# The branch ahead of a fused attention and expert kernel moved behind it, and the work planned anew

## The chip, the cores and the metric

The kernel runs on one core of one Trainium2 chip. The metric is the device time of one execution in microseconds; three timed executions of the kernel before gave a median of 732.55 us (731.89 to 733.72). Besides these there is one profiled execution, from which every number about single instructions comes.

## What is computed

The reference is an attention with a sliding window and a few global keys, followed by a gated product of two projections and an output projection:

```python
# q, k, v: (4, 8, 768, 64); n_global = 8, n_local = 96
scores = scale * np.matmul(q, k.transpose(0, 1, 3, 2))
is_global = pos[None, :] < int(n_global)
is_local = (rel >= 0) & (rel < int(n_local))      # rel = row - column
keep = is_global | is_local
dist = np.where(is_global & ~is_local, float(n_local), np.abs(rel))
scores = np.where(keep, scores - slopes * dist, -1e9)
a = softmax(scores)                               # with 1e-9 added to the sum
x = (a @ v) as 3072 rows of 512
out = ((x @ w_a) * (x @ w_b)) @ w_out             # d_ff = 1536
```

The two counts, n_global and n_local, are inputs of the program (64-bit integers in HBM), and so are the weights, which arrive as 64-bit floats and are turned into a high and a low float part on the chip. A program must therefore be right for other counts as well. The kernel has a fast path, which covers n_global up to 8 and n_local from 1 to 97, and a general path for everything else. The inputs of all runs here are covered by the fast path.

## The kernel before, in words

**The start.** `build` (L1401) loads the counts into a tile `nv` on SP's queue, and the first tile of packed queries and keys, `raw0`, in four pieces on the queues of SP and ScalarE (`build_first`, L1387). GpSimd writes positions, VectorE makes them into distances (`build_positions`, L1349). `load_flag` (L1341) has each of the five engines read the four 32-bit words of the counts from HBM into registers. `build_counts` (L1328) turns the 64-bit counts into floats on VectorE with four small operations (L1334 to L1337), and `build_masks` (L1374, six VectorE operations, L1379 to L1384) makes the two masked distance tiles `rel` and `col` with them. Then comes `tc.If(fast > 0)` (L1419): every engine works out the condition in its own registers and branches; the fast path is the first arm, the general path the `Else` arm (L1422).

**The fast path.** Its work is cut into eight units. Unit 0 holds the first block of 128 query rows of each of the four batches, the others two or three blocks each. For each unit there is an attention part, and then the projections (`moe`, L1000) in 12 steps, one for each 128 of d_ff. While unit u goes through its projections, the attention of unit u + 1 is done beside it. Unit 0's attention (`first`, L853) has nothing to hide beside. It goes through four pairs of heads in the order of `FIRST` = (1, 0, 2, 3); for each pair two `quad`s (L802), each of which has score matmuls on PE (L821), the subtraction of the scaled distances with a row minimum on VectorE (L659), the exponential on ScalarE (L676), a normalization (L708 or L710), a transposition on PE (L735), a copy out of PSUM, and the product with V (L787). Each head other than head 2 needs its own multiple of the two distance tiles; these are made by `scale_dists` (L635, one narrow and one wide operation for each head, L641), on VectorE or GpSimd. The weights of each of the 12 steps come as two loads on SP's queue (L473) and are converted by ScalarE and VectorE (`load_w`, L455), 768 columns at a time; the projections of unit 0 can't go on without them.

**What sets the order.** Every piece of work is an `Op` with a due time and a cost for each engine that can do it. `Schedule.order` (L266) plays the program through with these costs, gives each operation an engine where there is a choice, and writes down one order; the instructions are then emitted in exactly that order (`run`, L1121). The due times are first shifted at random by the numbers in `MOVES` (L79), each of which stands for one set of shifts, for operations of about the first two units. In the plan all engines are free at time 0.

**The first loads.** `fetch_first` (L541) gives the four raw tiles and the four V tiles of unit 0 due times ahead of everything else, each V tile next to its raw tile; they lie in memory that later holds the weights of the last steps (`w8` to `w11`). The weight tiles are in one pool (L407), and its memory starts where temporary tiles of the mask operations had been.

**The end.** The last unit's results are copied out of PSUM and stored by SP, and a last half by ScalarE's queue (L1113). Then each engine leaves the arm of the branch, past the general path, and all meet in a closing barrier (recorded at L1402).

Of the kernel before, what the change touches and what calls it, by code (L numbers as in the profile page):

```python
# [47 lines left out]

HOMES = "kk sm raw hh v wm hl xh xl o qh pf ql t"
PAD = 40  # L50
# [28 lines left out]
MOVES = (1010, 1025, 1037, 1048, 1089, 1106, 1156, 1251, 1276, 1371, 1475, 1603, 1662, 1754, 1881, 11792, 12402, 7, 26, 46, 60, 85, 142, 169, 213, 252, 392, 531, 549, 595, 835, 995, 2161, 2240, 11001)  # L79
TRACE = False  # L80
LAGS = {"pe": 200.0, "act": 270.0, "dve": 230.0, "pool": 290.0, "dma": 2300.0}
BIG = float(2**38)
# [143 lines left out]
class Schedule:  # L226
# [39 lines left out]
    def order(self, ops, dues):  # L266
# [5 lines left out]
        free = {e: 0.0 for e in self.SYNC}  # L272
# [36 lines left out]
        for op in ops:  # L309
            if not op.before:  # L310
                arrive(op)
        while len(out) < len(ops):
# [48 lines left out]
            elif kind == 1:  # L361
                arrive(op)
            else:
# [26 lines left out]
class Fast:  # L390
# [28 lines left out]
    def sbuf(self, shape, dtype, tag, name, bufs=1):  # L419
        return self.plan.buf(self.sp[tag], shape, dtype, tag, name, bufs=bufs)  # L420

# [33 lines left out]
    def load_w(self, f, due):  # L455
# [3 lines left out]
        for g in range(2):  # L459
            raw = self.plan.buf(self.wp, [P, 2 * WN], I32, f"w{f}_{g}", f"wr{f}_{g}")  # L460
            w = self.plan.buf(self.wp, [P, 2 * WN], F32R, f"w{f}_{g}", f"wt{f}_{g}")
# [79 lines left out]
    def fetch_first(self, c, due):  # L541

        pl = PLANS[0]
        v = self.plan.buf(self.wp, [P, 2 * WN], F32, f"w{NF - 1 - c}_1", f"v0_{c}")
        nv = 2 * pl.nv * D
        if c != FIRST[0]:
            raw = self.plan.buf(self.wp, [P, 2 * WN], F32, f"w{NF - 1 - c}_0", f"raw0_{c}")
# [87 lines left out]
    def scale_dists(self, h, due, wide):  # L635
        rel, col = self.dists
        b, n = self.negs[h // 4], (h % 4) * 3 * P
        for src, at, w, when in ((col, 2 * P, P, due), (rel, 0, 2 * P, wide)):
            self.plan.op(
                when,  # L640
                lambda e, src=src, at=at, w=w: self.engine(e).tensor_scalar_mul(  # L641
                    b[:, n + at : n + at + w], src[:, :w], 2.0 ** (2 - h)
# [5 lines left out]
                pool=pool(w) * 0.5,  # L648
            )
# [471 lines left out]
    def run(self):  # L1121
# [23 lines left out]
        with self.tc.manual_schedule():  # L1145
            for op in order:
# [181 lines left out]
def build_counts(nc, pool, nv):  # L1328

    words = nv.bitcast(I32).rearrange("p (n two) -> p n two", two=2)  # L1330
    low, high = words[:, :, 0], words[:, :, 1]
    nf = pool.tile([P, 2], F32, name="nf")
    t = pool.tile([P, 2], F32, name="nt")
    nc.vector.tensor_scalar(t, low, 0.0, None, op0=ALU.is_lt)  # L1334
    nc.vector.tensor_copy(nf, low)
    nc.vector.tensor_tensor(t, t, high, op=ALU.add)
    nc.vector.scalar_tensor_tensor(nf, t, float(2**32), nf, op0=ALU.mult, op1=ALU.add)  # L1337
# [3 lines left out]
def load_flag(nc, ns):  # L1341

    _, words = nc.values_load_multi_w_load_instructions(ns.bitcast(I32)[0:1, 0:4])
    g, g_high, l, l_high = words
    small = ((g >> 4) | g_high | (l >> 7) | l_high) == 0
    return small & (g <= G) & (l >= 1) & (l <= LW + 1)
# [54 lines left out]
def build(nc, a, out):  # L1401
    with tile.TileContext(nc) as tc, ExitStack() as ctx:  # L1402
        cp = ctx.enter_context(tc.tile_pool(name="c", bufs=1))
        with tc.manual_schedule(), tc.tile_pool(name="tmp", bufs=1) as tp:
# [3 lines left out]
            spare = cp.tile([P, PAD], F32, name="spare")  # L1408
            nc.gpsimd.memset(spare, 0.0)
            nc.scalar.activation(spare, spare, AF.Exp)  # L1410
# [8 lines left out]
        with tc.If(fast > 0) as branch:  # L1419
            with inner:  # L1420
                main.run()
# [75 lines left out]
```

## Time and profile before

| | |
|---|---|
| median of three runs | 732.55 us |
| the profiled execution's own time | 731.68 us |
| its span, first to last instruction | 729.8 us |
| mean granted clock of TensorE | 0.999 |
| busy: PE, VectorE, ScalarE, GpSimd | 708.6, 483.1, 353.1, 5.9 us |

In the rows of the profile PE is TensorE's matmuls, PEld its weight loads, DVE VectorE, ACT ScalarE, POOL GpSimd and SP SyncE. A q behind an engine's name (ACTq, SPq) means its sequencer, which issues DMAs, reads registers and branches; such records are not counted as busy. A row such as `8.38 0.40 ACT L676 ...` gives a start and a length in us, the engine and the line; what stands in brackets is how long the engine sat idle before it, and what ended that. A busy PE is not necessarily at its peak, since its matmuls overlap in their records.

### The profile page before, as it was taken

Reading aid. Unit: us, or ns where it says so; the run is one execution under the profiler, and the core shown is the slowest. Engines: PE = TensorE matmul, PEld = TensorE weight load, DVE = VectorE, ACT = ScalarE, POOL = GpSimd, SP = SyncE. Lnnn points to the kernel's source line nnn. Section 1 sums busy time; section 2 is a strip of 40 time slices with the busy share of each in tenths; the row PEclk is TensorE's granted clock in tenths of the full one; section 3 lists DMA queues with packets and bytes.
Section 4 is the critical chain, followed back from the end, with each engine's and each line's share of the span. In section 5 each row is a group of like instructions: output and inputs, shape, how many; then the busy total and the mean of one; then the engine's idle time right before and its main releaser. Section 6 shows DMA issues by size and latency. Waiting matters only on the chain.

```text
span 729.8 us, 12598 instructions
## 1 busy us (share of the span) xinstructions
PE 708.6 (97%) x4356; PEld 639.2 (88%) x4356; DVE 483.1 (66%) x1560; ACT 353.1 (48%) x907; POOL 5.9 (1%) x16
## 2 busy tenths in 40 slices
PE   5899999999999999999999999999999999999996
PEld 4577777899899999999899999998999999999996
DVE  6999999779975873587726967278662896321111
ACT  5999776364553552555426544263443554221111
POOL 3000000000000000000000000000000000000000
PEclk9999999999999999999999999999999999999999
DMA  7899100134543343134331343224432243110001
GB/s 269 316 380 364 41 17 28 42 101 127 170 137 81 90 129 108 64 89 125 89 104 65 106 129 108 65 85 106 135 101 86 65 128 88 45 44 1 1 1 48
DMA packets 38552, 78.06 MB, mean 107 GB/s; under 512 B 8528, under 2 KB 21072, under 8 KB 38480
## 3 DMA queue, kind: packets, MB, share of 16 engines
q1 hardware_dynamic: 28960, 67.33, 28.8%
q10 hardware_dynamic: 9520, 9.84, 5.3%
q8 instruction: 36, 0.59, 0.3%
q14 instruction: 36, 0.29, 0.1%
HBM read 51.97 MB, written 6.29 MB: 80 GB/s over the span
## 4 chain that ended last, share of the span: by engine, by line
PE 84%; DVE 5%; ACT 3%; DMA 3%; ACTq 2%; issue 1%; SPq 1%; DVEq 0%; POOL 0%; POOLq 0%
PE p L1042 49%; PE acc L1060 24%; PE pa L787 5%; PE ps L953 4%; DMA pf<-wm 3%; ACTq L766 2%; DVE t L659 1%; ACT t L676 1%; DVE wm L752 1%; ACT wr L516 1%; PE pt L735 1%; PE ps L821 1%; SPq L766 1%; DVE kk L447 1%; PE acc_2b L1060 1%
## 5 line engine op out<-in xcount | busy, mean ns | idle before, releaser
L1042 PE MATMUL p<-xh,wt 128*128 128x384 f32 (+2 forms) x1488 | 419.5, 337 | 1.4 <-ACT raw L437 0.9
L1042 PEld LDWEIGHTS p<-xh,wt 128*128 128x128 f32 x1488 | 271.0, 188 | 15.2 <-ACT raw L437 1.9
L1042 PE MATMUL p<-xl,wt 128*128 128x384 f32 (+2 forms) x816 | 269.7, 340 | 0.7 <-ACT xl L437 0.5
L1060 PE MATMUL acc<-wt,hh 128*128 128x512 f32 (+1 forms) x576 | 203.4, 390 | 0.0
L1042 PEld LDWEIGHTS p<-xl,wt 128*128 128x128 f32 x816 | 153.4, 188 | 10.8 <-ACT xl L437 0.8
L1060 PEld LDWEIGHTS acc<-wt,hh 128*128 128x128 f32 x576 | 108.3, 188 | 20.0 <-issue 1.6
L1081 DVE TENSOR_TENSOR raw<-p,raw 128x384 f32<-128x384 f32 (+2 forms) x96 | 52.9, 551 | 90.5 <-PE p L1042 89.7
L676 ACT ACTIVATE t<-t,sm 128x232 f32<-128x232 f32 (+1 forms) x120 | 55.3, 464 | 116.7 <-DMA pf<-wm 71.3
L1060 PE MATMUL acc<-wt,hl 128*128 128x512 f32 (+1 forms) x288 | 111.7, 388 | 0.0
L437 ACT COPY raw<-p 128x384 f32<-128x384 f32 (+2 forms) x71 | 34.4, 485 | 122.3 <-PE p L1042 116.2
L447 DVE TENSOR_TENSOR hl<-raw,hh 128x384 fp32r<-128x384 f32 (+2 forms) x96 | 52.8, 550 | 11.1 <-ACT hh L437 10.4
L1060 PEld LDWEIGHTS acc<-wt,hl 128*128 128x128 f32 x288 | 54.2, 188 | 6.6
L659 DVE CUSTOM_DVE_ANT_0 t<-ps,rel 128x232 f32<-128x232 f32 x74 | 28.8, 389 | 39.2 <-PE ps L953 38.4
L447 DVE TENSOR_TENSOR kk<-raw,kk 64x348 fp32r<-64x348 f32 x96 | 49.6, 516 | 3.6 <-ACT kk L437 0.5
L437 ACT CAST hh<-raw 128x384 fp32r<-128x384 f32 (+2 forms) x72 | 37.3, 519 | 19.8 <-DVE raw L1081 19.6
L787 PE MATMUL pa<-pf,v 128*64 128x128 f32 x640 | 41.5, 278 | 1.7 <-ACT pf L437 1.4
L787 PEld LDWEIGHTS pa<-pf,v 128*64 128x64 f32 x640 | 35.9, 138 | 7.2 <-issue 3.5
L953 PE MATMUL ps<-kk,qh 128*128 128x232 f32 x144 | 39.8, 277 | 1.5 <-DVE sm L659 1.5
L708 ACT ACTIVATE wm<-wm,sm 128x232 f32<-128x232 f32 x58 | 27.9, 487 | 24.6 <-DVE sm L698 23.9
L953 PE MATMUL ps<-kk,ql 128*128 128x232 f32 x144 | 39.5, 274 | 0.0
L676 ACT ACTIVATE wm<-wm,sm 128x232 f32<-128x232 f32 x72 | 34.7, 483 | 5.7 <-DVE sm L659 5.1
L708 ACT ACTIVATE t<-t,sm 128x232 f32<-128x232 f32 (+1 forms) x76 | 34.6, 477 | 5.1 <-DVE sm L698 4.0
(84 smaller groups left out, 687.4 us busy)
## 6 DMA issues: line engine op xcount, KB each, us to landing
wr<-wts SPq DMA_DIRECT2D x24, 768.0 KB, 10.9
raw<-qkv SPq DMA_DIRECT2D x48, 366.0 KB, 3.0
v<-qkv SPq DMA_DIRECT2D x24, 384.0 KB, 3.2
pf<-wm ACTq DMA_DIRECT2D x192, 48.0 KB, 2.0
pf<-wm SPq DMA_DIRECT2D x192, 48.0 KB, 1.9
out<-o SPq DMA_DIRECT2D x23, 256.0 KB, 2.0
v<-qkv SPq DMA_DIRECT2D x8, 256.0 KB, 3.9
raw<-qkv SPq DMA_DIRECT2D x3, 512.0 KB, 8.0
```

What stands on the lines that cost most here:

```text
L437: self.nc.scalar.copy(out(), src())
L447: lambda e: self.engine(e).tensor_sub(out(), a(), b()),
L516: lambda e, low=low: nc.scalar.activation(low(), low().bitcast(U32), AF.Copy, scale=2.0**-29),
L659: lambda e, j=j, o=o, w=w, neg=neg, at=at: nc.vector.tensor_tensor_reduce(t[:, o : o + w], ps[:, o : o + w], neg[:, at : at + w], -scale, ...
L676: lambda e, j=j, o=o, w=w: nc.scalar.activation(t[:, o : o + w], t[:, o : o + w], AF.Exp, bias=sm[:, j : j + 1], scale=-1.0, accum_out=sm[ ...
L708: nc.scalar.mul(t[:, o : o + w], t[:, o : o + w], r)
L766: lambda e, out=out, src=src: self.queue(e).dma_start(out(), src()),
L787: nc.tensor.matmul(pa[D * s : D * s + D, i * P : i * P + P], v[:, v0 : v0 + D], probs[s, i][1](c), start=c == 0, stop=c == len(slots) - 1,)
L953: nc.tensor.matmul(ps[:, :w], q[:, i * P : i * P + P], kk[:, k0 : k0 + w], start=m == 0, stop=m == 1,)
L1042: nc.tensor.matmul(p[:, :T], wt(), b[:, b0 : b0 + T], start=c == 0 and n == 0, stop=c == NCC - 1 and n == 2,)
L1060: nc.tensor.matmul(acc[:, :n], hs[:, i * P : i * P + P], wt(), start=f == 0 and k == 0, stop=f == NF - 1 and k == 2,)
L1081: lambda e, asb=asb, pb=pb: nc.vector.tensor_mul(asb[:, :T], pb[:, :T], asb[:, :T]),
```

## The change

The test moves from ahead of the fast path to behind it, and a few things that hang on that are changed with it:

- `load_flag` and the branch at the start are gone. The fast path is emitted without a condition.
- The masks take only the lower words of the counts, by one cast (`build_low`); the high words no longer enter the masks.
- When 95% of the plan's operations have been emitted, `late()` puts in seven small VectorE operations which make the full counts and one flag in SBUF, and has ScalarE, VectorE, GpSimd and SP read the flag into a register. TensorE reads it behind its last matmul.
- Behind the fast path stands `tc.If(flag == 0)` with the general path in it, told to fall through on the side where the condition is false. For counts that aren't covered the general path writes the output again.
- The plan knows at which times the engines become free (`BEGIN`), ScalarE may do the scaling of the distances, the V tiles' due times lie two loads later, and `MOVES` has 15 other numbers in place of 35. The plan's order is thereby another one throughout.
- Every weight tile has its own pool; the pools are opened with the tiles of step 4 first, and those of steps 0 to 3 last.
- The operand of the first exponential, which only loads its table, is one column of the limits tile and not a tile of 40 columns.

```diff
+BEGIN = {"pe": 4700.0, "act": 5200.0, "dve": 5100.0, "pool": 5200.0, "dma": 2400.0}
...
-        free = {e: 0.0 for e in self.SYNC}
+        free = dict(BEGIN)
...
+        for n, at in enumerate(sorted(BEGIN.values())):
+            heappush(heap, (at, 3, n, None))
...
-        self.wp = ctx.enter_context(tc.tile_pool(name="w", bufs=1))
+        tags = [f"w{(f + 4) % NF}_{g}" for f in range(NF) for g in range(2)]
+        self.wp = {tag: ctx.enter_context(tc.tile_pool(name=tag, bufs=1)) for tag in tags}
...
-            due + 1, lambda e: self.copy_in(v, nv, VOFFS[0][c]), writes=[v], dma=nv * 4 * P / 360.0
+            due + 2 * LOAD + 1,
+            lambda e: self.copy_in(v, nv, VOFFS[0][c]),
...
-                lambda e, src=src, at=at, w=w: self.engine(e).tensor_scalar_mul(
-                    b[:, n + at : n + at + w], src[:, :w], 2.0 ** (2 - h)
+                lambda e, out=out, src=src, by=2.0 ** (2 - h), w=w: (
+                    self.nc.scalar.mul(out(), src[:, :w], by)
+                    if e == "act"
+                    else self.engine(e).tensor_scalar_mul(out(), src[:, :w], by)
                 ),
...
+                act=act(w),
...
-            for op in order:
+            for n, op in enumerate(order):
+                if n == int(LATE * len(order)):
+                    late()
                 op.emit(op.engine)
...
+def build_low(nc, pool, nv):
+    nf = pool.tile([P, 2], F32, name="low")
+    nc.vector.tensor_copy(nf, halves(nv)[0])
+    return nf
...
+class Covered:
...
+    def early(self):
+        self.counts()
+        v, ok = self.nc.vector, self.ok
+        v.tensor_tensor(ok, self.nf, self.lim, op=ALU.is_le)
+        v.scalar_tensor_tensor(
+            ok[:, 0:1], self.nf[:, 1:2], 1.0, ok[:, 0:1], op0=ALU.is_ge, op1=ALU.mult
+        )
+        v.tensor_mul(self.flag, ok[:, 0:1], ok[:, 1:2])
+        self.handles = self.load([e for e in mybir.ALL_ENGINES if e != mybir.EngineType.PE])
+
+    def value(self):
+        handles = self.handles + self.load([mybir.EngineType.PE])
+        return self.nc.snap(bass.RegisterHandles(handles))
...
-            fast = load_flag(nc, a["ns"])
-            nf = build_counts(nc, cp, nv)
-            build_masks(nc, rel, col, first, t, nf)
-        inner = ctx.enter_context(ExitStack())
-        main = Fast(inner, tc, a["qkv"], a["wts"], out, raw0, (rel, col, ident))
-        with tc.If(fast > 0) as branch:
-            with inner:
-                main.run()
-        with branch.Else():
+            build_masks(nc, rel, col, first, t, build_low(nc, cp, nv))
+        covered = Covered(nc, cp, nv, lim)
+        with ExitStack() as inner:
+            Fast(inner, tc, a["qkv"], a["wts"], out, raw0, (rel, col, ident)).run(covered.early)
+        with tc.If(covered.value() == 0, preferred_fallthrough_block=False):
             with ExitStack() as inner:
-                General(
-                    inner, tc, a["qt"], a["kt"], a["v"], a["wts"], out, (nf, ident)
-                ).run()
+                General(inner, tc, a["qt"], a["kt"], a["v"], a["wts"], out, (covered.nf, ident)).run()
```

More of the change, by code (lines that the diff above doesn't have):

```diff
@@ L49 @@
 HOMES = "kk sm raw hh v wm hl xh xl o qh pf ql t"
-PAD = 40
 START = 52000
@@ L1325, in run, with halves @@
             self.batch(b)
-def build_counts(nc, pool, nv):
+def halves(nv):
     words = nv.bitcast(I32).rearrange("p (n two) -> p n two", two=2)
[L1331 to L1337, printed above, removed]
-    return nf
@@ L1341, in load_flag, with build_limits @@
[L1341 to L1346, printed above, removed]
+    return words[:, :, 0], words[:, :, 1]
+def build_low(nc, pool, nv):
+    nf = pool.tile([P, 2], F32, name="low")
+    nc.vector.tensor_copy(nf, halves(nv)[0])
+    return nf
+def build_limits(nc, pool):
+    lim = pool.tile([P, 2], F32, name="lim")
+    nc.gpsimd.memset(lim[:, 0:1], float(G))
+    nc.gpsimd.memset(lim[:, 1:2], float(LW + 1))
+    return lim
```

43 lines of the change are left out of this document (33 added, 10 removed).

## The prediction

> **What bounds the kernel now.** I read the page's head first, then the busy time by stages, then the first microseconds in order of time, then the tail and the waits of TensorE.
>
> ```profile
> span 729.8 us, 12598 instructions
> ```
> ```profile
> 0.00:5.00 5.00, 0.00 (x0) 0.00 (x0) 1.58 (x9) 1.52 (x2) 1.30 (x10) 1.00 0.49 105
> 5.00:10.00 5.00, 2.90 (x23) 2.65 (x24) 4.08 (x29) 1.62 (x9) 4.17 (x5) 1.00 0.66 228
> 10.00:15.00 5.00, 4.46 (x28) 3.03 (x26) 4.05 (x31) 4.11 (x20) 0.09 (x1) 1.00 1.02 376
> 15.00:41.00 26.00, 21.15 (x146) 13.71 (x146) 25.26 (x100) 26.00 (x80) 0.37 (x1) 1.00 0.85 325
> 41.00:60.00 19.00, 18.78 (x95) 15.02 (x96) 19.00 (x41) 19.00 (x35) 0.00 (x0) 1.00 1.01 407
> 60.00:120.00 60.00, 60.00 (x298) 47.10 (x297) 59.23 (x113) 45.24 (x83) 0.00 (x0) 1.00 0.28 102
> 200.00:690.00 490.00, 488.45 (x3049) 455.80 (x3048) 294.98 (x1004) 207.03 (x559) 0.00 (x0) 1.00 0.31 89
> ```
> In the second fence the columns behind the stretch and its length are the busy times of PE, PEld, DVE, ACT and POOL, then the granted clock, the DMA share and GB/s. From 41 us on PE is the bound: it idles 0.22 us to 60, nothing to 120, and 1.55 us in the 490 behind 200. Before 41 it is not: it is busy 28.51 of 41 us. There VectorE and ScalarE are full from 15 us on (25.26 and 26.00 of 26), with the softmax of the first unit and the first weights' conversion. So what the change can win at the front is what it lets these two engines start earlier; the long middle belongs to PE and its work is untouched. The third place is behind PE's last matmul.
>
> **The front, step by step.**
>
> ```profile
> 0.74 0.39 SPq L1406 DMA_DIRECT2D nv<-ns  x1
> ...
> 1.19 1.20 SPq L1397 DMA_DIRECT2D raw<-qkv  x2
> ...
> 3.79 0.17 DVE L1334 TENSOR_SCALAR nt<-nv 128x2 f32<-128x2 int32 x1 [2.07 <-DMA nv<-ns]
> ...
> 4.19 0.16 DVE L1337 SCALAR_TENSOR_TENSOR nf<-nt,nf 128x2 f32<-128x2 f32 x1
> 4.47 0.34 DVE L1379 TENSOR_SCALAR after<-rel,nf 128x224 f32<-128x224 f32 x1
> ...
> 5.09 2.08 PE L821 MATMUL ps<-raw 64*128 64x128 f32 x16 [5.09 <-DMA raw<-qkv]
> ...
> 5.50 0.35 SPq L562 DMA_DIRECT2D raw<-qkv  x1
> ...
> 6.55 1.77 DVE L641 TENSOR_SCALAR negs<-col 128x128 f32<-128x128 f32 x7 [0.92 <-DVE col L1384]
> ...
> 8.04 0.28 DVE L659 CUSTOM_DVE_ANT_0 t<-ps,col 128x128 f32<-128x128 f32 x1
> ...
> 8.38 0.40 ACT L676 ACTIVATE t<-t,sm 128x128 f32<-128x128 f32 x1 [4.85 <-DVE sm L659]
> ...
> 9.80 0.64 DVE L641 TENSOR_SCALAR negs<-rel 128x256 f32<-128x256 f32 x2
> ```
> ```profile
> L1419 DVEq ALU_OP  x12: 47/53/58, 5.5 to 6.4; - x12
> ...
> L1419 ACTq COMPARE_BRANCH  x2: 45/46/47, 4.8 to 724.4; - x2
> L1419 PEldq COMPARE_BRANCH  x2: 92/1914/3737, 4.9 to 721.2; - x2
> L1419 SPq COMPARE_BRANCH  x2: 43/48/53, 5.1 to 724.5; - x2
> L1419 DVEq COMPARE_BRANCH  x2: 55/56/57, 6.4 to 723.5; - x2
> ```
> The first fence is the timeline (start, duration in us, engine, line; in brackets the idle time before and what ended it), the second the source view of the branch (ns, minimum, median and maximum; then first and last start).
>
> *The branch on VectorE.* It does its twelve register operations and its compare only when its masks are issued, from 5.5 to 6.4 us, and the 0.92 us of idle time at 6.55 is that. All of it goes.
>
> *The counts.* Today the masks wait for three further operations: the cast at the second place, then L1336, then L1337, and L1379 starts 0.28 us behind L1337's start. With the cast alone L1379 starts 0.28 us after the cast. The cast can start where L1334 starts now, 3.79, so L1379 at 4.07 and not 4.47: 0.40 us earlier. The four operations with the high words go to the last unit, below.
>
> So VectorE is free at 6.55 − 0.92 − 0.40 = 5.23 us, 1.32 us earlier. Seven narrow scalings stand before its first L659 today. If they all stay, L659 starts at 8.04 − 1.32 = 6.72. If they don't, the scores are the bound: PE starts at 5.09 for the landing of raw, its 16 records for the two quads last 2.08 us, so the first quad is there at 5.09 + 1.04 = 6.13. The first L659 thus moves by 1.32 to 1.91 us. I take 1.8: ScalarE, which may now do scalings, sits idle until 8.38, and the first two L659 read the unscaled distance, so little need stand ahead.
>
> *The nine scalings on VectorE* (1.77 + 0.64 = 2.41 us) may go to ScalarE. What ScalarE does before its first exponential costs nothing; that is 8.38 − 1.8 = 6.6 less 5.2, so 1.4 us, or four or five of them at the 0.40 of an activation of this size. What is taken from VectorE helps by at most half, since copies and normalizations can then be shared anew between two full engines: 0 to 1.2 us, and I take 0.6 as half the scalings move. If ScalarE does them later than its first exponential, they cost it 0.4 each and the term is nought or below: with seven of them behind it, 2.8 − 1.2 = 1.6 us lost.
>
> *The first loads.*
>
> ```profile
> SPq L562 <- DVE rel L1382: 0.3, 1, 0.3
> ```
> SP has issued raw0 at 1.19 + 1.20 = 2.39 us, then reads the counts and branches, and issues its next load at 5.50, the last 0.3 us of it waiting for a mask operation whose memory the load's tile takes over. The weight pools are now opened with w4 ahead, so that this memory falls to a tile that is loaded later. So the load can come at 2.4, with the V tiles each behind the next raw tile. PE waits for a load once, at the very start; no later idle row of it in these 41 us names one. So 3.1 us earlier loads are worth nothing by themselves; they are what keeps up with softmax work that starts 1.8 us sooner, in a stretch where DMA is at 1.02. PE's own start stays at 5.09: it waits for raw0, whose issue isn't moved.
>
> Front: 1.8 + 0.6 = 2.4 us; bounds 1.3 − 1.6 = −0.3 and 1.9 + 1.2 = 3.1.
>
> **The test at 95%.** Seven VectorE operations on 128x2 (0.16 to 0.17 each by the rows above, 1.2 us), and a register read on four engines that waits for them.
>
> ```profile
> 699.96 0.48 ACT L437 COPY raw<-p 128x384 f32<-128x384 f32 x1 [4.55 <-PE p L1042]
> ...
> 700.55 0.56 DVE L1081 TENSOR_TENSOR raw<-p,raw 128x384 f32<-128x384 f32 x1 [4.56 <-PE p L1042]
> ```
> ```profile
> L1343 SPq TENSOR_LOAD <-ns x1: 503/503/503, 3.7 to 3.7; - x1
> ...
> L1343 PEldq TENSOR_LOAD <-ns x1: 1762/1762/1762, 1.8 to 1.8; - x1
> ```
> Queued behind the waiting read are ScalarE's copy of p, VectorE's product and, on SP, stores. In the last unit's steps both engines idle 4.55 us of each; 1.2 and a read of 0.5 to 1.8 us fit (4.55 − 3.0 = 1.5 left), so 0. Without that cover PE would lose up to 3.0 us once. PE's own read comes behind its last matmul.
>
> **The tail.**
>
> ```profile
> L1402 SPq EVENT_SEMAPHORE  x8: 17/28/28, 728.6 to 729.7; - x8
> ...
> L1402 DVEq DRAIN  x2: 10/34/57, 726.8 to 729.3; - x2
> L1402 ACTq DRAIN  x2: 8/38/67, 728.5 to 729.3; - x2
> ```
> ```profile
> 723.98 0.39 ACTq L1113 DMA_DIRECT2D out<-o  x1
> ```
> ```profile
> L1113 SPq DMA_DIRECT2D out<-o x24: 332/343/502, 152.1 to 724.0; - x24
> ```
> ```profile
> out<-o ACTq DMA_DIRECT2D x1, 128.0 KB, 3.1
> out<-o SPq DMA_DIRECT2D x1, 128.0 KB, 3.4
> ```
> The path ends with the last stores: 723.98 + 3.1 = 727.1, and on SP 724.0 + 3.4 = 727.4. But the engines leave the fast arm by jumping over the general path, and then nothing is recorded for a while: VectorE from its compare at 723.5 to 726.8, ScalarE from 724.4 to 728.5, SP from 724.5 to 728.6, and PE's jump itself is a record of 3.74 us. VectorE has no store to wait for, and its gap is 3.3 us, so this is the jump and not the landing. SP and ScalarE are done with it 1.2 us behind the landing, and the closing barrier then takes 729.8 − 728.6 = 1.2. With the general path behind and the covered side falling through, the barrier can begin at 727.4: 1.2 us gained; 0 if a jump remains. I take 1.2, because all four gaps have one size, whether a store stands before them or not.
>
> [...]
>
> **Sum.** 2.4 + 0 + 1.2 = 3.6 us. The profiled execution took 731.68 us (its span 729.8, and 1.9 around it), so 728.1; the median of the runs is 732.55, 0.87 above it, so 728.95, say 729.0.
>
> **The rivals.**
>
> *A. The exit still jumps.* Then ScalarE and SP fetch after their last store as today, and only the front is left: 732.55 − 2.4 = 730.2. For it: the general path has to lie somewhere. Against: the test names the side that falls through. If a wait for the stores also came ahead of such a jump, the end would be 727.4 + 4.1 + 1.2 = 732.7 of span, 2.9 later, and front and tail nearly cancel at 733.0. Together 0.14. [...]
>
> *B. The front is not won.* PE becomes the bound at 41 us only because two engines are full till then, and VectorE stays full to 120. If scalings on ScalarE land among its exponentials (2.8 us, above), only the tail is left: 732.55 − 1.2 = 731.4. For it: ScalarE is the fuller one from 15 to 41. Against: the new start times let it do them before 6.6 us. 0.13.
>
> *C. Slower: the order written anew makes PE wait in the middle.* Other start times and other shifts of due times give another order over the first two units' 24 steps.
>
> ```profile
> 41.22 0.50 PE L1042 MATMUL p<-xh,wt 128*128 128x512 f32 x1 [0.65 <-ACT raw L437]
> ```
> ```profile
> PE ps L953 <- DVE sm L659: 1.5, 3, 0.7
> PE p L1042 <- ACT raw L437: 0.3, 1, 0.3
> PE p L1042 <- DVE raw L439: 0.2, 1, 0.2
> ```
> The first is what one such wait costs: a copy that stood behind a weight conversion on a full ScalarE, 0.65 us. Six of them eat the gain (3.6 / 0.65); with one in half the steps, 12, it is 732.55 − 3.6 + 7.8 = 736.8. For it: both engines are full while PE is at 19 of 19. Against: from 42 to 720 us the order of now has five such waits, 2.0 us (second fence). 0.09.
>
> *D. Better.* A new order can also remove these 2.0 us, and with the front at 3.1 it is 732.55 − 3.1 − 1.2 − 2.0 = 726.2. 0.06.
>
> **How the numbers follow.** The forecast has 0.58. What can be told from no change is 0.3%, or 2.2 us: below 730.35 is faster, above 734.75 slower. Faster: 0.55 of the forecast (0.03 where the front comes out at its lower end), 0.08 of A, all of D: 0.69. Slower: 0.08 of C. Same: the rest, 0.23. The range runs from 726.0 (just under D) to 732.8, which takes in A's and B's times and most of what an idle front leaves; C and the worst of A are outside, with half of D, about 2 in 10.
>
> **What would show it.** Right: no idle second of VectorE behind the masks, its first L659 at about 6.2 and the first exponential at 6.6 us; SP's second raw load at 2.4; PE's unbroken stretch from about 38.8 and not 41.2; the end some 4.6 us behind the last store's issue rather than 5.8. Wrong: a first exponential at 6.6 and PE's stretch still from 41 means that ScalarE or VectorE has taken on as much as it won (B); a gap of 3 to 4 us on an engine behind the last store is A; idle rows of PE between 42 and 200 us above 5 us in all is C; an idle row of PE around 650 us that names ScalarE or VectorE means that the test isn't covered.

## The result, and the profile after

The changed kernel takes 737.43 us (median of seven executions, 735.08 to 740.32), the kernel before 732.55 us beside it (seven, 730.51 to 734.83). The ratio is 1.0064, 95% interval 1.0039 to 1.0089: slower by 4.9 us, where 729.0 was forecast. The profiled execution of after took 736.5 us, 4.8 more than the one of before: 4.4 of that are in the span, 0.4 around it.

The head of the page, and the busy time by stages (columns as in the prediction):

```profile
span 734.2 us, 12555 instructions
```
```profile
0.00:5.00 5.00, 0.17 (x2) 0.17 (x3) 1.92 (x10) 1.55 (x3) 1.52 (x12) 1.00 0.64 114
5.00:10.00 5.00, 3.38 (x28) 3.02 (x30) 4.10 (x29) 4.16 (x19) 2.28 (x3) 1.00 0.92 350
10.00:15.00 5.00, 4.04 (x22) 2.44 (x22) 3.34 (x25) 3.55 (x13) 0.00 (x0) 1.00 1.03 416
15.00:41.00 26.00, 22.65 (x147) 14.51 (x146) 24.65 (x98) 24.82 (x78) 0.00 (x0) 0.93 0.84 331
41.00:60.00 19.00, 18.43 (x84) 14.63 (x83) 18.98 (x40) 19.00 (x35) 0.00 (x0) 1.00 0.99 391
60.00:120.00 60.00, 60.00 (x309) 46.93 (x308) 59.45 (x112) 45.94 (x81) 0.00 (x0) 1.00 0.25 90
200.00:690.00 490.00, 489.04 (x3052) 456.58 (x3052) 297.15 (x1019) 208.35 (x566) 0.00 (x0) 1.00 0.32 89
```

The first two rows show more work than before in them (ScalarE 4.16 us of 5 from 5 to 10, where it had 1.62). The third and fourth show where it stops: from 10 to 15 us ScalarE is busy 3.55 us where it was 4.11 and VectorE 3.34 where it was 4.05, and from 15 to 41 neither is full any more (24.82 and 24.65, before 26.00 and 25.26). From 41 us on little differs. So the loss is ahead of 42 us and behind the last matmul. The timeline of after, with the front's steps and with the start of PE's unbroken stretch:

```profile
2.44 0.59 SPq L575 DMA_DIRECT2D v<-qkv  x1
3.06 0.43 SPq L575 DMA_DIRECT2D raw<-qkv  x1
...
3.46 0.17 DVE L1357 CAST low<-nv 128x2 f32<-128x2 int32 x1 [1.75 <-DMA nv<-ns]
...
4.93 0.71 ACT L656 ACTIVATE negs<-col 128x128 f32<-128x128 f32 x3 [1.45 <-DVE col L1443]
4.94 0.83 DVE L658 TENSOR_SCALAR negs<-col 128x128 f32<-128x128 f32 x4
...
6.08 0.29 DVE L676 CUSTOM_DVE_ANT_0 t<-ps,col 128x128 f32<-128x128 f32 x1 [0.31 <-PE ps L838]
...
6.42 0.40 ACT L693 ACTIVATE t<-t,sm 128x128 f32<-128x128 f32 x1 [0.47 <-DVE sm L676]
...
8.69 2.08 PE L838 MATMUL ps<-raw 64*128 64x128 f32 x16 [1.62 <-DVE sm L715]
...
10.70 0.90 PE L752 MATMUL pt<-ident,t 128*128 128x128 f32 x3
11.43 0.37 ACT L446 COPY pf<-pt 128x256 f32<-128x256 f32 x1 [1.57 <-PE pt L752]
11.53 0.29 DVE L676 CUSTOM_DVE_ANT_0 t<-ps,negs 128x128 f32<-128x128 f32 x1 [1.96 <-PE pt L752]
...
42.48 0.50 PE L1059 MATMUL p<-xh,wt 128*128 128x512 f32 x1 [0.56 <-ACT raw L446]
```

The first exponential is at 6.42 us, 1.96 earlier than the 8.38 of before, and the stretch starts at 42.48 us, 1.26 later than 41.22. Between the two ScalarE has lost 3.2 us. The row of its copy at 11.43 shows the largest piece: PE does 16 score matmuls of the next pair of heads (8.69) ahead of the first transpositions (10.70), and ScalarE and VectorE wait 1.57 and 1.96 us for these.

The tail: the rows of the last copy and store, the source view of the branch (L1477), that of the closing barrier (L1461; the columns are count, ns, first and last start), and the landings (the last column is us from issue to landing).

```profile
724.11 1.53 SPq L1130 DMA_DIRECT2D out<-o  x3
...
724.89 0.42 DVE L1120 COPY o<-acc_2b 128x256 f32<-128x256 f32 x1 [2.41 <-PE acc_2b L1077]
725.35 0.36 ACTq L1130 DMA_DIRECT2D out<-o  x1
```
```profile
L1477 SPq EVENT_SEMAPHORE  x8: 17/17/17, 725.9 to 729.6; - x8
...
L1477 SPq COMPARE_BRANCH  x2: 43/46/49, 725.8 to 729.6; - x2
```
```profile
L1477 POOLq COMPARE_BRANCH  x2: 38/42/45, 650.0 to 650.1; - x2
```
```profile
L1461 SPq EVENT_SEMAPHORE  x10: 17/28/28, 732.9 to 734.2; - x10
...
L1461 POOLq DRAIN  x3: 34/82/117, 650.6 to 734.0; - x3
```
```profile
out<-o SPq DMA_DIRECT2D x1, 128.0 KB, 3.8
```

SP compares at 725.8 us and does not go over to the general path. Then it waits eight times, until the last stores have landed (ScalarE's at 725.35 + 3.9 = 729.25); the last wait is at 729.6, and only now comes its second branch. It can only be the jump past the general path, of which nothing is recorded. The next record is at 732.9: 3.3 us in which nothing is recorded. (GpSimd, which has nothing left to do from 650 us on, jumps at 650.1 and has its next record at 650.6, 0.5 us later.) Before, the jump came first (724.5) and the landing of the stores (727.4) lay inside its gap, which ended at 728.6. So the landing and the jump stand in series now. From the start of the last copy (724.89) to the end it is 9.3 us; before it was 729.8 − 723.52 = 6.3.

The account of the 4.4 us: front 1.26; middle (stretch to last copy) 724.89 − 42.48 = 682.41 against 682.30, so 0.1; tail 3.0. This is one trace of each. A second trace of the kernel before, shown at the end of the experiments, starts its stretch at 42.04, has 682.58 us to the last copy and ends 5.8 us behind that. Against it the front costs 0.4, the middle −0.2 and the tail 3.5.

### The profile page after: what moved, and what is told of

The parts are those of the page before. It is cut to its first block, busy times and chain, and to the rows that moved or that the text cites. A ratio compares the mean times of both kernels' runs of the same rounds, so it can differ in the third digit from the quotient of the medians.

```text
span 734.2 us, 12555 instructions
## 1 busy us (share of the span) xinstructions
PE 711.8 (97%) x4356; PEld 640.8 (87%) x4356; DVE 484.4 (66%) x1564; ACT 354.7 (48%) x910; POOL 3.8 (1%) x14
## 4 chain that ended last, share of the span: by engine, by line
PE 84%; DVE 6%; ACT 3%; DMA 2%; ACTq 1%; issue 1%; SPq 1%; DVEq 0%
PE p L1059 49%; PE acc L1077 24%; PE pa L804 5%; PE ps L970 4%; DMA pf<-wm 2%; ACTq L783 1%; PE ps L838 1%; DVE kk L456 1%; PE pt L752 1%; DVE t L676 1%; DVE wm L769 1%; ACT wr L526 1%; ACT t L693 1%; PE acc_2b L1077 1%; SPq L783 1%
## 5 line engine op out<-in xcount | busy, mean ns | idle before, releaser
L693 ACT ACTIVATE t<-t,sm 128x232 f32<-128x232 f32 (+1 forms) x120 | 55.1, 461 | 117.7 <-DMA pf<-wm 96.9
L970 PE MATMUL ps<-kk,ql 128*128 128x232 f32 x144 | 39.5, 275 | 0.0
L676 DVE CUSTOM_DVE_ANT_0 wm<-ps,rel 128x232 f32<-128x232 f32 x72 | 28.1, 391 | 12.7 <-PE ps L970 12.5
```

The source lines that it names most:

```text
L676: lambda e, j=j, o=o, w=w, neg=neg, at=at: nc.vector.tensor_tensor_reduce(t[:, o : o + w], ps[:, o : o + w], neg[:, at : at + w], -scale, ...
L693: lambda e, j=j, o=o, w=w: nc.scalar.activation(t[:, o : o + w], t[:, o : o + w], AF.Exp, bias=sm[:, j : j + 1], scale=-1.0, accum_out=sm[ ...
L970: nc.tensor.matmul(ps[:, :w], q[:, i * P : i * P + P], kk[:, k0 : k0 + w], start=m == 0, stop=m == 1,)
```

## The experiments

My theories were: the exit's order (first the waits, then a jump) costs about 3 us, and the new order of unit 0's work takes back what the earlier start wins. The rivals: a jump costs the same wherever it stands, and the loss of the front comes from the clock or from ScalarE's scalings. Where no other is named, the ratios are to the kernel before beside them (732.2 to 732.6 us, 22 to 35 executions).

### The general path as the side that falls through

```diff
-        with tc.If(covered.value() == 0, preferred_fallthrough_block=False):
+        with tc.If(covered.value() == 0, preferred_fallthrough_block=True):
```

> The changed kernel, with the test told to fall through into the general path, so that the covered side jumps over it first and waits for the stores behind the jump. Exit theory (in the changed kernel each engine first waits for the stores and then jumps, so landing and fetch stand one behind the other): the span ends about 6.3 us behind the last matmul's start of its final record group as in the kernel before, not 9.3, and the time falls by about 3 us to 734.4. Rival (the fetch comes behind the stores in either layout, or the extra time is the register reads): still 9 us behind, 737.4. The front stays as in the changed kernel in both, PE's unbroken stretch from about 42.5.

Measured: 734.18 us (12 executions), ratio 1.0025 (1.0012 to 1.0039), 3.3 us below after. The source view of the branch, of the barrier, and the stores:

```profile
L1477 SPq EVENT_SEMAPHORE  x8: 17/17/17, 729.4 to 729.9; - x8
...
L1477 SPq COMPARE_BRANCH  x1: 45/45/45, 726.9 to 726.9; - x1
```
```profile
L1461 SPq EVENT_SEMAPHORE  x10: 17/28/28, 730.0 to 731.2; - x10
```
```profile
724.03 2.72 SPq L1130 DMA_DIRECT2D out<-o  x3
```

There is now one branch record on SP, and it comes ahead of the waits: the compare at 726.9 is the jump, and behind it, at 729.4, the stores have landed and the eight waits pass in 0.5 us. The last copy to the end is 731.3 − 724.81 = 6.5 us, near the 6.3 and 5.8 of the two traces of the kernel before. So the side that the test names as falling through isn't the one that costs nothing. The order of jump and waits was 3 us of the loss.

### No test at all

```diff
-            Fast(inner, tc, a["qkv"], a["wts"], out, raw0, (rel, col, ident)).run(covered.early)
-        with tc.If(covered.value() == 0, preferred_fallthrough_block=False):
-            ...
+            Fast(inner, tc, a["qkv"], a["wts"], out, raw0, (rel, col, ident)).run(lambda: None)
```

> The changed kernel without the test, the flag and the general path: it leaves out the path for counts that aren't covered. Exit theory: no jump and no fetch, the closing barrier follows the landing at once; the span ends 4.5 to 5.2 us behind the last matmul instead of 9.3, so the time falls by 4.2 to 4.8 us, to about 733. Rival (the closing barrier and the stores take the time, not the jump): it falls by under 1 us. The front stays, PE's stretch from about 42.5.

Measured: 731.07 us (10), ratio 0.9984 (0.9966 to 1.0002), 6.4 us below after and 3.1 below the kernel with the better exit. Its stores, landing and barrier:

```profile
724.65 1.52 SPq L1130 DMA_DIRECT2D out<-o  x3
```
```profile
out<-o SPq DMA_DIRECT2D x1, 128.0 KB, 2.1
```
```profile
L1461 SPq EVENT_SEMAPHORE  x7: 17/28/28, 728.2 to 729.2; - x7
```

The last copy (725.44) to the end is 3.8 us. What is missing against after's 9.3 is the jump (3.3), the eight waits (about 0.4 once the last store is there), and something that I had not priced: the last store of SP lands 2.1 us behind its issue, where it takes 3.8 in after and 3.4 in before. The fall of 6.4 us is thus more than the 4.2 to 4.8 that I expected. In the kernel above, where the landing takes 2.7, the three issues last 2.72 us and not 1.52 as here. So leaving out the test and the general path gains more than the gap behind the jump: the landing is earlier or the issues are shorter. That the jump does this is a guess that no run separates.

### The order of before, with each exit

Two kernels have the changed program but the plan of before: the 35 old shift numbers, all engines free at time 0, the V tiles' old due times, no scalings on ScalarE. On PE, ScalarE, VectorE and SP the fast path's operations then come, in the traces too, in the order of the kernel before.

```diff
-BEGIN = {"pe": 4700.0, "act": 5200.0, "dve": 5100.0, "pool": 5200.0, "dma": 2400.0}
+BEGIN = {"pe": 0.0, "act": 0.0, "dve": 0.0, "pool": 0.0, "dma": 0.0}
-MOVES = (30, 74, 125, ...
+MOVES = (1010, 1025, 1037, ...
-            due + 2 * LOAD + 1,
+            due + 1,
-                act=act(w),
```

> The changed kernel with the order of the kernel before on every engine (times of the engines at 0, the 35 old shifts, V due with its raw tile, no scaling on ScalarE); still no branch in front, the cast alone, and the test behind. Order theory (what the earlier start wins is lost to the new order, which puts the second pair's 16 score matmuls ahead of the first transposes and leaves ScalarE and VectorE idle for 2 us): the first exponential at about 7.0, PE's unbroken stretch from 39.5 to 39.9 instead of 42.5, the time about 734.5 with the exit as in the changed kernel. Rival (the earlier start itself does it: loads that come sooner crowd DMA, or PE stays slow for longer): PE's stretch from 41.2 or later whatever the order, the time 736 to 737.5.

> Both of these edits together: the old order, no branch in front, and the test falling through into the general path. If both theories hold, the front is 1.3 to 1.9 us earlier than in the kernel before and the exit equal to it: 730.6 to 731.3 against 732.55. If only the exit theory holds, 733 to 734.5; if only the order theory holds, 734.5; if neither, 737.

Measured: with after's exit 734.92 us (12), ratio 1.0032 (1.0020 to 1.0044), 2.5 below after; with the general path falling through 732.19 us (12), 0.999 (0.9976 to 1.0004), 2.0 below its counterpart in the new order. The better exit is worth 2.7 us in this pair and 3.3 in the first. The second of them was run again later: 731.67 us (12), 0.9986 (0.9973 to 1.0). Both times lie above the 730.6 to 731.3 that I expected if both theories held; the section on the kernel before once more has what the traces show of that.

> The same program as the one with the order of before and the better exit (732.19 us, 0.999 of the kernel before), run again beside its counterpart with the hint. Theory 1, the hint gains on the path: this one is 0.7 us or more above the counterpart. Theory 2, the 0.95 us between the two earlier times was scatter between calls of one and the same middle: within 0.5 us of each other, both 731 to 732.5.

The timeline of the later run, its first exponential and the start of the stretch:

```profile
6.72 0.40 ACT L692 ACTIVATE t<-t,sm 128x128 f32<-128x128 f32 x1 [3.24 <-DVE sm L675]
...
39.95 0.50 PE L1058 MATMUL p<-xh,wt 128*128 128x512 f32 x1 [0.64 <-ACT raw L446]
```

The exponential comes 0.3 us later than in after and the stretch 2.5 us earlier: 33.2 us lie between the two (before 32.8, after 36.1). So the old order keeps most of the earlier start, and the new one gives away more than it. The waits of ScalarE behind 8 us say how, in after and then in this kernel (us in total, times, longest):

```profile
ACT pf L446 <- PE pt L752: 2.8, 3, 1.6
```
```profile
ACT pf L446 <- PE pt L751: 0.8, 1, 0.8
```

In the first experiment's kernel, which has the same new order as after, the same wait comes to 1.8 us. So the new order has 1.0 to 2.0 us more of it.

And in the groups of ScalarE's instructions from the first exponential to the stretch, one more piece of weight conversion has come ahead of the copy that lets PE go on (before, then after; behind the first bar the busy us and the mean ns, behind the second the idle us):

```profile
L516 ACT ACTIVATE wr<-wr 128x768 int32<-128x768 uint32 x7 | 6.7, 952 | 0.0
```
```profile
L526 ACT ACTIVATE wr<-wr 128x768 int32<-128x768 uint32 x8 | 7.2, 916 | 0.0
```

The old order in the changed program has seven of them again. With this most of the 3.2 us that ScalarE lost is accounted for. Its idle time grew by 2.1 us (36.06 − 33.05 against 32.84 − 31.95, stretch less busy time) and its busy time by 1.1, of which the added conversion, 0.92 us long, is the larger part.

The trace of the run with after's exit speaks less clearly: its stretch starts at 41.59 us and not at the 39.5 to 39.9 expected. The granted clock has a dip in it, of which the section on the kernel before once more tells.

### The second pair's scores behind the first transpositions

```diff
+        turn = next(op for op in order if "turn" in kind(op))
+        scores = [op for op in order if "quad" in kind(op)][3]
+        order.remove(scores)
+        order.insert(order.index(turn) + 1, scores)
```

This is the kernel with the new order and the better exit (734.18 us), and one group of eight score matmuls moved.

> The changed kernel's new order with the mended exit (734.2 without this edit) and one operation moved on TensorE: the score matmuls of the second pair's second quad come behind the first two transposes and not ahead of them, as in the kernel before. Order theory, narrow form (this one place makes the idle time at 10 us): ScalarE's 0.8 to 1.6 us of idle time there is gone and PE's unbroken stretch starts about 1.2 us earlier, near 41; the time near 733. Wide form (it is the sum of many places: about 1 us more of ScalarE's work ahead of the stretch and several waits): the hole closes, but PE's stretch moves by under 0.5 us and the time stays within 733.7 to 734.5.

Measured: 733.55 us (12), ratio 1.0012 (0.9998 to 1.0025). This can't be told from 1.0025, and the trace shows no gain: the stretch starts later than the 41.86 of the unmoved kernel, and the waits only changed their place.

```profile
ACT pf L446 <- PE pt L752: 2.9, 4, 1.0
```
```profile
43.05 0.50 PE L1059 MATMUL p<-xh,wt 128*128 128x512 f32 x1 [0.58 <-ACT raw L446]
```

So the hole on ScalarE that starts at 9.86 us in after (the 1.57 us) is not by itself the cause; without it four shorter waits come to 2.9 us. The narrow form is thereby out. The wide form has the closed hole right, but the stretch moved by 1.2 us, to later, and the time lies just below its range.

### No scalings on ScalarE

```diff
-                act=act(w),
```

The rest is again the new order and the better exit.

> The changed kernel with the better exit (734.2 us), and ScalarE may not scale distances; everything else of the new order stays. Theory 1, the new shift numbers carry the loss: the hole of 1.6 us on ScalarE behind the first exponentials stays, and the time is within 0.7 us of 734.2. Theory 2, the scalings on ScalarE carry it: about 1.0 us less work on ScalarE before TensorE's unbroken stretch, which starts at 41.3 or below, and 1 to 2 us gained. Theory 3, the numbers fit only the plan they were drawn for: no better, 734 to 737.

Measured: 732.96 us (12), ratio 1.0011 (0.9994 to 1.0027), which overlaps its counterpart's 1.0012 to 1.0039. In the trace the front isn't any earlier:

```profile
6.50 0.40 ACT L692 ACTIVATE t<-t,sm 128x128 f32<-128x128 f32 x1 [3.00 <-DVE sm L675]
...
42.62 0.50 PE L1058 MATMUL p<-xh,wt 128*128 128x512 f32 x1 [0.66 <-ACT raw L446]
```

ScalarE idles 3.00 us ahead of the exponential, which comes at the same time as with the scalings, and the stretch starts within the range of the kernels that have them (41.86 to 42.84). So ScalarE's scalings neither win nor cost anything that the trace shows. The median is 1.2 us below its counterpart, as theory 2 had it, and the stretch speaks against that theory; with overlapping intervals, taken beside different runs of the kernel before, a small cost of the scalings isn't excluded. In after itself ScalarE does four scalings, all between 4.93 and 5.95 us, ahead of its first exponential. The granted clock is 1.00 from 20 to 40 us here, so the late start doesn't need a lower clock either.

### The old shift numbers in the new plan

```diff
-MOVES = (30, 74, 125, ...
+MOVES = (1010, 1025, 1037, ...
```

Start times, costs and due times stay new; the exit is the better one.

> The changed kernel with the better exit (the covered side falls through, 734.2 us) and with the 35 shift numbers of the kernel before; the start times, ScalarE's scalings and the V tiles' due times stay new. Theory 1, the 15 new numbers carry the order's loss: the plan is near the old one, ScalarE waits for the transposes less than 1.5 us ahead of TensorE's unbroken stretch, which starts below 41.3 us (42.48 and 41.86 with the new numbers), and the time is 1.5 to 2.5 us under 734.2. Theory 2, the loss comes with the scalings that ScalarE does: nothing won, 733.5 to 735. Theory 3, each set of numbers fits only the plan it was drawn for, with its own start times and costs: any other pairing is no better than either, 734 to 737.

Measured: 746.01 us (5), ratio 1.0172 (1.0150 to 1.0194), 12 us above its counterpart with the 15 new numbers and outside all three theories. The busy time by stages shows PE losing time where it had none to lose:

```profile
41.00:60.00 19.00, 16.23 (x69) 11.85 (x69) 18.72 (x40) 18.22 (x33) 0.00 (x0) 1.00 1.01 408
60.00:120.00 60.00, 56.24 (x272) 42.66 (x270) 59.27 (x109) 43.10 (x73) 0.00 (x0) 0.94 0.23 79
```

From 60 to 120 us PE gets through 272 records where it did 309, at a granted clock of 0.94 instead of 1.00, and its jump at the end comes 15 us later than in after (738.7 against 723.6). So these 35 shifts, which serve the old plan well, serve this one badly. The slower rival of the prediction, an order that makes PE wait among the first two units, is real: from 42 to 200 us PE's waits come to 7.9 us here, against 1.2 in after. The 15 numbers of the change avoid it behind 42 us, and not ahead.

### The old order without the test

This is the second and the third edit together; it leaves out the test and the general path.

> The old order, no branch in front, and neither test nor general path (it leaves out the path for counts that aren't covered). If order and exit simply add: the run without a test (731.1) less the 2.0 to 2.5 us that the old order was worth, 728.6 to 729.1. Its middle tells whether the 1.4 us by which the run with the old order and the mended exit was ahead from 11 to 170 us is always given back between 170 and 200 us (theory: the exchange by DMA there makes it up each time) or was so by chance (then it is kept in this run).

Measured: 729.38 us (5), ratio 0.9956 (0.9941 to 0.9972). It is the only kernel of the study that is faster by over 0.3%, and it isn't whole: it shows what an exit without a jump would give. It comes 0.3 us above the 728.6 to 729.1 of a plain sum. As for the question about the middle: against before, compared at like operations of ScalarE, this run loses 1.1 us between 142 and 201 us. The two traces of the old order with the better exit lose 1.3 and 0.4 there, the two traces of the next section at most 0.1. So the loss there is not a constant of the order.

### A hint ahead of the last branch

The kernel with the old order and the better exit, and behind the reading of the flag, some 75 us ahead of the branch, a hint on each engine but PE that says whether the branch will be taken.

```diff
+        rest = [e for e in mybir.ALL_ENGINES if e != mybir.EngineType.PE]
+        self.handles = self.load(rest)
+        taken = self.nc.snap(bass.RegisterHandles(self.handles)) == 0
+        self.tc.mark_branch_hint_location("test", taken, rest)
```

> The run with the old order and the exit jump ahead of the wait (732.2), with a prefetch hint for that jump added on ScalarE, VectorE, GpSimd and SP at 95% of the plan, behind the read of the flag (not on TensorE, which reads its flag last). Exit theory (what is left at the exit is the fetch behind the jump, 3.3 to 4.1 us on each engine, 2.5 us of it on the path, as the run without any jump showed: 3.8 us from its last copy's start to the end against 6.3): the gap between jump and next record on SP and ScalarE falls below 1 us, and the time by up to 2.5 us, to about 729.8, under both kernels. Rival (a hint does nothing across so many instructions, or takes room from the sequential fetch): no change or slower, 732 to 734.

> The same program as the one with the order of before, the better exit and the hint ahead of the last branch (731.24 us, 0.9984 of the kernel before), run again beside its counterpart without the hint. Theory 1, the hint gains on the path: last copy's start to the end below 6.0 us, and 0.7 us or more under the counterpart. Theory 2, it does not: 6.5 to 6.9 us again, and within 0.5 us of the counterpart.

Measured: 731.24 us (9), ratio 0.9984 (0.9973 to 0.9995), and in the repetition 731.24 us (12), 0.998 (0.9965 to 0.9995), where the same kernel without the hint has 731.67 and 0.9986 (0.9973 to 1.0). The branch in the repetition with the hint, then in the one without:

```profile
L1480 DVEq COMPARE_BRANCH  x1: 90/90/90, 721.1 to 721.1; - x1
L1480 DVEq EVENT_SEMAPHORE  x1: 21/21/21, 721.7 to 721.7; - x1
L1480 ACTq COMPARE_BRANCH  x1: 76/76/76, 722.0 to 722.0; - x1
...
L1480 ACTq EVENT_SEMAPHORE  x1: 17/17/17, 724.9 to 724.9; - x1
```
```profile
L1476 DVEq COMPARE_BRANCH  x1: 72/72/72, 724.0 to 724.0; - x1
L1476 ACTq COMPARE_BRANCH  x1: 58/58/58, 724.8 to 724.8; - x1
...
L1476 DVEq EVENT_SEMAPHORE  x1: 21/21/21, 727.5 to 727.5; - x1
L1476 ACTq EVENT_SEMAPHORE  x1: 17/17/17, 727.6 to 727.6; - x1
```

VectorE's gap falls from 3.5 to 0.6 us; ScalarE's stays (2.9 and 2.8), and so does SP's (2.5 and 2.6), which ends last. The last copy to the end is 6.6 us with the hint and 6.1 without, and in the first pair 6.8 and 6.7. So the hint did its work on an engine that nobody waits for, and nothing on the path. That the two medians lie 0.4 us apart is not shown to be the hint's doing.

### The kernel before once more

> The kernel before once more, for a second trace of the same program: how far do two profiled executions of one program differ along their matmuls? If by under 0.3 us at every place, then the 0.4 to 1.1 us that the runs with the old order lose between 170 and 200 us belong to the edit; if by about 1 us, they are the scatter of that place.

Measured: 732.3 us (one execution). It is the same program as before, and its stretch starts 0.8 us later:

```profile
42.04 0.50 PE L1042 MATMUL p<-xh,wt 128*128 128x512 f32 x1 [0.65 <-ACT raw L437]
```

That is how far one trace of this front can be trusted. Further on the second trace is 0.2 to 1.3 us behind the first at like operations of ScalarE, so differences of about 1 us in the middle are scatter.

The old order shows this best. From the start of the stretch to the last copy it takes 683.7 to 684.3 us in its four traces without a hint and 681.1 and 681.2 in the two with one, though their instructions are the same until 646 us; the two traces of the kernel before have 682.30 and 682.58, the new order 682.4 to 683.2. So the 1.0 to 1.4 us by which the old order's stretch starts earlier are less than what the middle scatters. In the two traces with the better exit and no hint the last copy starts at 724.18 and 723.90 us, no earlier on the whole than the 723.52 and 724.62 of the kernel before. What the old order is worth has to be read from the medians.

In the second trace of the kernel before, as in after, the granted clock has a dip (0.66 from 30 to 35 us; in after 0.66 from 35 to 40). Seven of the fourteen profiles have one, of either order, so the dip isn't of the change. The two old-order kernels whose profiles have it start the stretch at 41.59 and 41.11 us, against 39.87 to 40.19 in the four that don't. The new order starts at 41.86 to 43.05 in all five, with it or without.

## Why the prediction was wrong

**The earlier start: right.** Forecast were a first subtraction at 6.2 us, a first exponential at 6.6 and SP's second raw load at 2.4. They came at 6.08 and 6.42, and SP's first load behind raw0 at 2.44. That load is a V tile, though, and the raw tile follows at 3.06, the other way round than forecast. VectorE goes from the masks to the scalings without a gap and then waits 0.31 us for the scores. Part of this is luck: the cast of the counts was to start at 3.79 as before and starts at 3.46. It does so at 3.45 to 3.61 in all traces without the branch in front, against 3.79 and 3.75 in the two with it; the prediction had no term for that.

**The test at 95%: right.** The seven operations took 0.16 us each between 648.15 and 649.3, the readings of the flag 0.48 to 0.54 us, and the middle is 0.1 us longer in all.

**The step "front: 1.8 + 0.6 = 2.4 us": wrong from the moment it was summed.** The 1.8 was the gain at the first exponential (1.96 measured), and I carried it over to PE's stretch 35 us later as if the order between them were the same. It isn't the same: ScalarE needs 3.2 us more for that stretch, for 2.1 us more of idle time, nearly all of it waits on transpositions, and for one conversion. Instead of 2.4 us won, 1.26 are lost in the trace. The medians say the same: with the better exit the new order is still 1.6 us above the kernel before (734.18 against 732.58). With the old order the start of the stretch moved by 1.0 to 1.4 us in the four profiles without a dip, and the old order is 1.7 to 2.5 us better in three pairs of kernels that differ in the plan alone. The term of 0.6 for the scalings doesn't show: VectorE kept seven of its nine, without any on ScalarE the stretch starts at 42.62, and the "four or five" that were to fit into 1.4 us at 0.40 each are three. So rival B came in by its outcome, and not by its reason (scalings among the exponentials), which that run speaks against. Which operations make the new order worse ahead of 42 us stays open. Two single places, the hole at 9.86 us and the scalings, were tried and neither is it alone.

**The step "1.2 us gained with the covered side falling through": wrong in sign, and the larger part of the miss.** It rested on the sentence that the test names the side that falls through. It names it, but by the records the side that falls through here is only a short block that waits for the stores and then jumps over the general path, and the code behind it lies beyond that path. The text had the case, as rival A's worst form (a wait for the stores ahead of such a jump, 2.9 us later), and its price was right: 3.0. The price was in part luck: the waits ended 4.7 us behind the start of the last copy and not 3.9, and the gap behind the jump was 3.3 us and not 4.1. Its sign, a gap of 3 to 4 us behind the last store, is there, and the end comes 8.9 us behind the last store's issue, where 4.6 was forecast. What was wrong was its chance. "The general path has to lie somewhere" was the whole argument, and it holds for either side: a jump past the general path is needed on whichever arm does not run into it. The rows show a gap in both layouts (3.3 us on SP behind the jump in after, 2.5 behind the compare with the general path falling through). In the traces of before and after, packets of the two DMA queues marked instruction start in these long gaps: four (0.04 MB) between 729.9 and 730.6 us in that of SP in after, five (0.05 MB) between 724.7 and 727.5 in that of SP in before (724.5 to 728.6), and none in GpSimd's 0.5 us of either. Over the whole span the two queues have 36 and 36 packets (36 and 35 with the hint), and 34 and 29 or 30 in the two kernels without a branch. So instructions are loaded while the engines have no record; that these wait for the load is a guess that no run separates, and for which engine a packet comes isn't recorded. What decides the time is what is put inside that gap, the landing of the stores or nothing (6.5 and 9.3 us from the last copy to the end). A smaller reading of the prediction doesn't hold: its four gaps of one size leave out GpSimd, whose gap is 0.5 us.

**Rival C, an order that makes PE wait in the middle: not here.** Behind 42 us PE's waits come to 2.1 us, as against 2.0 before. The old numbers in the new plan show that such an order exists and what it can cost: 7.9 us of PE's waits from 42 to 200 us.

The two wrong steps make up the difference: 2.4 + 1.26 and 1.2 + 3.0 are 7.9 us of the 8.0 between the forecast gain of 3.6 and the 4.4 lost in the span, in this one pair of traces. With both put right in the way that keeps the general path, the old order and the better exit, the time is 732.19 and 731.67 us: at best level with the kernel before (0.999 and 0.9986). With the hint it is 731.24 both times (0.9984 and 0.998), 0.2% below the kernel before, and how much of that is the hint's is not shown.

## What to carry to other kernels

A branch moved from the front to the back doesn't lose its jump: ask, for the arm that runs, which records stand between its last store and the closing barrier, and let the jump come ahead of the wait for the stores and not behind it (2.7 and 3.3 us in the two pairs here). A gain at the first instruction of a stretch counts only if the order behind it is the same one; where an edit also makes a new plan, cost the plan by its waits up to the point where the next bound begins, or change it by itself. Numbers that suit one plan need not suit the next: the 35 shifts that belong to the better order here cost 12 us in a plan with other start times and costs. And one trace of each kernel can make an account come out to 0.1 us where a second trace of the same program moves its parts by 0.3 to 0.8 us.

## What the runs showed of the hardware

- Behind a jump past the general path VectorE, ScalarE and SP have no record for 2.5 to 4.4 us (without a hint), though the jump's own record lasts 0.04 to 0.09 us; on PE the record itself is 3.6 to 4.3 us long. On GpSimd the gap is 0.4 to 0.5 us in every trace with a jump; why it is so much shorter was not tested. Which side is named as falling through didn't remove the jump: the gap is there on SP with either one (3.3 us in after, 2.5 with the general path falling through).
- The last stores land later in the kernels whose engines jump: SP's last one 3.0 to 4.0 us behind its issue in before (twice), in after and in the old order with after's exit, 2.1 us in both kernels without a branch. With the general path falling through, it landed after 2.5 to 3.9, and SP's last issues took longer as well (three of them 2.2 to 3.0 us, against 1.5 to 1.7). The runs don't show by what.
- A hint given 75 us ahead took away nearly all of VectorE's gap (3.5 to 0.6 us), and nothing of ScalarE's or SP's. Why only there stays open.
- Two profiles of one and the same program differed by 0.8 us in when PE's stretch starts, and a dip of the granted clock to 0.66 to 0.74, as the mean of five microseconds, came between 20 and 40 us in seven of the fourteen profiles, with either order; of the two profiles of the kernel before one has it and one hasn't.
